# Attention output and adapters with head dims on partitions, sums of the softmax by a stationary matrix of ones

## The chip, the cores and the metric

One core of one Trainium2 chip runs the whole kernel. The metric is the device time of one execution in microseconds (us). The engines are TensorE (PE, with its weight loads PEld), VectorE (DVE), ScalarE (ACT), GpSimd (POOL) and SyncE (SP); each works through its own queue in order.

## What is computed

Banded attention for 8 batch rows, 8 heads, 576 positions and head size 64, and then a mixture of low-rank adapters on the 4608 resulting rows of 512 numbers:

```python
scores = scale * np.matmul(q, k.transpose(0, 1, 3, 2))
mask_plain = (rel >= 0) & (rel < window)                      # window 32, heads 0 to 3
mask_dil = (rel >= 0) & (rel < window * dilation) & (rel % dilation == 0)   # dilation 4, heads 4 to 7
attn = np.exp(scores - max)
attn = attn / (np.sum(attn, axis=-1, keepdims=True) + 1e-09)
x = np.matmul(attn, v)                                        # then to rows of 8 heads x 64
...
logits = x @ w_gate                                           # 8 experts
topk = np.argpartition(-logits, K, axis=1)[:, :K]             # the best 2
w = softmax over the two
delta[mask] += w[mask, k, None] * ((x[mask] @ A[e]) @ B[e])   # rank 16
return x + delta
```

## The kernel before

The host reorders q, k, v so that the dilated heads become banded heads too (positions sorted by their class modulo 4). A batch row is then two groups g of four heads, and within a group two pairs xy of two heads. Keys lie in 9 blocks of 64, and a block meets at most 96 queries, so a score tile has 64 keys on partitions and 96 queries along the row.

For each batch row r (there are 8) the steps are, by the names that the plan gives them:

- loads `g`, `q`, `v`: q, k and v of one group and half, from float32 in memory to bf16 in the tile `kv`, 64 partitions each, issued on POOL. Three slots of `kv` are used in turn.
- S0, S1: masks and scores of a group by small matmuls into two banks each; E0, E1: the exponential on ACT, from PSUM to the tile `p` (bf16). Keys are on partitions.
- Va, Vb (line 612): for a pair of heads, values. `p` is the stationary operand, 128 queries wide, and v of two heads is the moving one, 65 columns each: 64 of v and a column of ones that the host put there, whose product is the sum of the softmax. So the result has queries on partitions, and each query's sums are single columns. H (line 657) does the same for the last 64 positions of all eight heads.
- R and RH (lines 635, 677): the reciprocals of those columns on DVE; N and NH: the product of values and reciprocals, on DVE, from PSUM to the output tile `x` in float32. N frees the banks of the pair.
- B and BH: casts of `x` to bf16 on POOL (tiles `xb`, `xbh`). T0, T1, TH: transposes on PE by the identity, so that head dims lie on partitions; C0, C1, CH: copies of the transposes on ACT to the tile `xt`.
- Z0, Z1: gate and first adapter matrices, `xt` stationary; ZC: copies to `zs` on ACT; M, s12, tt, th, top, g2: the choice of the best two and their weights (DVE, and a tanh on ACT); gz: weighted products on POOL.
- GT: transposes of gz on PE; gc and gn: two copies of them, in class order on DVE and in natural order on ACT. D: the second adapter matrices, gn and gc stationary, `bt` moving; A: the addition to `x` on DVE. For the names in `VIA` the addition goes by a copy to `tmp` on ACT (AC) and an addition on POOL (AP).
- st: stores of finished columns of `x`, issued on SP behind the loads.

The order on every engine is written out by hand in the string `ORDER`. A name with `@n` also says which PSUM bank, of eight, it starts in. `replay` only reads it; the costs given to `add` (for example `dve(60)` for R) set nothing but the filler matmuls. Instructions are recorded by a wrapper, so all stand at line 124 in the profile; they are told apart by their tiles.

```python
ve.reciprocal(rec, o[:, :, D : D + VW + 1 : VW])        # R: 8 numbers per partition
...
ve.reciprocal(RECH[r % 2], o[:, :, D])                  # RH: 4 numbers per partition
```

Of the kernel before, what the change touches and what calls it, by code (L numbers as in the profile page):

```python
# [10 lines left out]
FP = mybir.dt.float32  # L11
# [13 lines left out]
PER = 192  # L25
CI = S // C
VW = D + 1
# [5 lines left out]
KV = 2 * VN + QN  # L33
# [17 lines left out]
VIA = ("4 4", "4 5", "4 6", "3 7")  # L51
GT2 = (7,)
# [3 lines left out]
startACT aw land_aw startPOOL startSP con land_con bt land_bt startDVE pz11 pz31 table pz10 g011 land_g011  # L56
zero00 g010 land_g010 q000 land_q000 zero10 btc q001 land_q001 v000 land_v000 v001 land_v001 md S0_0.1@0 pz20
pz00 g100 land_g100 E0_0.1 S1_0.1@2 zero01 Va_0.2@0 E1_0.1 Vb_0.2 g101 land_g101 pz01 xz1 awc S0_0.0@2 E0_0.0
R_0.2 xz0 N_0.2 g110 land_g110 pz21 g111 land_g111 gz00 g200 land_g200 S1_0.0@4 E1_0.0 Va_0.0@2 g201 land_g201
Vb_0.0 zero11 gz01 R_0.0 N_0.0 Va_0.3@4 Vb_0.3 R_0.3 N_0.3 Va_0.1@0 Vb_0.1 R_0.1 N_0.1 H_0@2 RH_0 g211  # L60
land_g211 S0_1.0@4 E0_1.0 g210 land_g210 S1_1.0@0 E1_1.0 B_0.0 pz30 B_0.2 NH_0 B_0.3 B_0.1 T1_0@3 C1_0 T0_0@2
Va_1.0@4 Va_1.1@6 g301 land_g301 C0_0 Vb_1.0 R_1.0 N_1.0 Vb_1.1 R_1.1 N_1.1 BH_0 TH_0@3 CH_0 S0_1.1@0 E0_1.1
g300 land_g300 Z0_0@3 ZC0_0 M0_0 g310 land_g310 Z1_0@6 ZC1_0 M1_0 zero20 S1_1.1@0 E1_1.1 s12_0 B_1.0 top_0
Va_1.2@2 tt_0 th_0 Va_1.3@6 g2_0 B_1.1 zero21 T0_1@4 C0_1 Vb_1.2 R_1.2 Vb_1.3 N_1.2 R_1.3 S0_2.0@0 E0_2.0
H_1@5 S1_2.0@2 gz0_0 E1_2.0 GT_0@4 Va_2.1@0 N_1.3 B_1.3 Va_2.0@6 RH_1 NH_1 BH_1 gc_0 gn_0 Vb_2.1 R_2.1 TH_1@2
CH_1 N_2.1 B_1.2 Vb_2.0 R_2.0 N_2.0 T1_1@3 C1_1 D2p_0@4 A2p_0 S0_2.1@0 E0_2.1 S1_2.1@6 g311 land_g311 E1_2.1
B_2.0 Z1_1@3 ZC1_1 M1_1 g400 land_g400 Z0_1@2 ZC0_1 M0_1 g401 land_g401 g410 land_g410 Va_2.3@4 Va_2.2@6
Vb_2.3 R_2.3 s12_1 g411 land_g411 top_1 B_2.1 N_2.3 B_2.3 Vb_2.2 R_2.2 S0_3.0@2 tt_1 N_2.2 H_2@0 RH_2 E0_3.0
NH_2 BH_2 S1_3.0@4 th_1 g2_1 T0_2@1 gz0_1 E1_3.0 C0_2 Va_3.1@2 D4_0@6 A4_0 Vb_3.1 R_3.1 N_3.1 B_3.1 Va_3.0@4
B_2.2 TH_2@0 CH_2 Vb_3.0 R_3.0 D0p_0@6 N_3.0 A0p_0 S0_3.1@2 E0_3.1 GT_1@0 g501 land_g501 g500 land_g500  # L70
S1_3.1@4 E1_3.1 g510 land_g510 T1_2@1 gc_1 gn_1 Va_3.2@6 Va_3.3@2 Vb_3.2 R_3.2 N_3.2 Vb_3.3 C1_2 D0p_1@4 A0p_1
R_3.3 N_3.3 B_3.0 T0_3@0 g511 land_g511 C0_3 Z0_2@1 ZC0_2 Z1_2@6 ZC1_2 M0_2 M1_2 s12_2 S0_4.0@4 E0_4.0 H_3@1
top_2 RH_3 NH_3 B_3.2 tt_2 S1_4.0@2 E1_4.0 D2p_1@6 A2p_1 B_3.3 T1_3@4 Va_4.0@0 C1_3 Va_4.1@2 BH_3 TH_3@5 CH_3
th_2 g2_2 Vb_4.0 R_4.0 N_4.0 Vb_4.1 R_4.1 N_4.1 S0_4.1@6 E0_4.1 Z0_3@5 ZC0_3 g601 land_g601 M0_3 Z1_3@4 ZC1_3
M1_3 s12_3 tt_3 S1_4.1@6 E1_4.1 top_3 th_3 gz0_2 GT_2@5 Va_4.3@2 gc_2 g2_3 Va_4.2@0 D4_1@4 A4_1 gn_2 Vb_4.3
R_4.3 N_4.3 Vb_4.2 g610 land_g610 R_4.2 N_4.2 S0_5.0@6 H_4@5 E0_5.0 RH_4 NH_4 S1_5.0@2 E1_5.0 gz0_3 GT_3@4
gc_3 gn_3 B_4.0 D0p_2@6 A0p_2 B_4.3 D2p_2@0 A2p_2 S0_5.1@2 E0_5.1 B_4.1 T0_4@5 Va_5.0@6 D4_2@4 A4_2 Vb_5.0
R_5.0 C0_4 g600 land_g600 S1_5.1@2 E1_5.1 Va_5.1@0 N_5.0 B_4.2 T1_4@5 C1_4 g611 land_g611 BH_4 TH_4@4 Vb_5.1
CH_4 R_5.1 N_5.1 Va_5.3@2 Va_5.2@6 Vb_5.3 R_5.3 N_5.3 Vb_5.2 D0p_3@4 A0p_3 R_5.2 g700 land_g700 Z0_4@0 Z1_4@1
ZC1_4 N_5.2 M1_4 ZC0_4 M0_4 top_4 B_5.3 s12_4 tt_4 g710 land_g710 B_5.2 S0_6.0@2 E0_6.0 H_5@4 RH_5 NH_5  # L80
S1_6.0@0 E1_6.0 S0_6.1@6 E0_6.1 D2p_3@2 A2p_3 T1_5@5 Va_6.1@0 g711 land_g711 g701 land_g701 B_5.1 BH_5 D4_3@4
A4_3 S1_6.1@6 B_5.0 Vb_6.1 C1_5 th_4 g2_4 gz0_4 Va_6.0@4 E1_6.1 R_6.1 N_6.1 TH_5@2 CH_5 T0_5@3 C0_5 Vb_6.0
R_6.0 N_6.0 Va_6.2@6 Va_6.3@0 GT_4@2 gc_4 gn_4 st_0 land_st_0 Vb_6.3 R_6.3 Vb_6.2 R_6.2 N_6.3 N_6.2 Z1_5@4
Z0_5@5 ZC1_5 M1_5 D4_4@0 ZC0_5 M0_5 S0_7.1@2 AC4_4 s12_5 tt_5 th_5 H_6@6 D2p_4@0 RH_6 NH_6 E0_7.1 S0_7.0@4
E0_7.0 S1_7.0@6 E1_7.0 top_5 A2p_4 D0p_4@2 g2_5 A0p_4 B_6.3 B_6.2 T1_6@0 C1_6 Va_7.0@4 BH_6 TH_6@1 Va_7.1@6 fz
Vb_7.0 R_7.0 B_6.1 Vb_7.1 CH_6 S1_7.1@2 E1_7.1 AP4_4 st_3 land_st_3 R_7.1 B_6.0 T0_6@1 gz0_5 N_7.1 N_7.0 C0_6
GT_5@0 gc_5 gn_5 B_7.0 Va_7.2@6 Va_7.3@2 Vb_7.2 R_7.2 Vb_7.3 R_7.3 N_7.2 N_7.3 Z0_6@1 ZC0_6 M0_6 B_7.1 Z1_6@0
ZC1_6 T0_7@6 C0_7 M1_6 s12_6 B_7.2 H_7@1 D4_5@0 RH_7 tt_6 B_7.3 T1_7@2 th_6 C1_7 NH_7 D2p_5@4 BH_7 TH_7@1 CH_7
top_6 g2_6 gz0_6 D0p_5@6 A2p_5 Z0_7@1 A0p_5 GT_6@4 gc_6 AC4_5 ZC0_7 Z1_7@5 ZC1_7 M0_7 gn_6 D2p_6@4 M1_7 s12_7
tt_7 th_7 top_7 g2_7 A2p_6 D4_6@1 AP4_5 AC4_6 st_5 land_st_5 D0p_6@6 A0p_6 gz0_7 gz3_7 GTn_7@6 gn_7 AP4_6 st_6  # L90
land_st_6 GT_7@7 gc_7 D3_7@7 AC3_7 D2_7@6 A2_7 st_7c land_st_7c D4_7@4 D0p_7@0 AP3_7 A4_7 st_7b land_st_7b
A0p_7 st_7a land_st_7a
# [234 lines left out]
def attn_adapters_kernel(  # L327
# [24 lines left out]
    XB = [[sb([128, 4, 128], BF, f"xb{i}{h}") for h in range(4)] for i in range(2)]  # L352
    XBH = [sb([128, 256], BF, f"xbh{i}") for i in range(2)]
# [3 lines left out]
    GN = [sb([128, 640], BF, f"gn{i}") for i in range(2)]  # L357
    GC = [sb([128, 640], BF, f"gc{i}") for i in range(2)]
    REC = [sb([128, 4, 2], FP, f"rec{i}") for i in range(3)]
    RECH = [sb([128, 4], FP, f"rech{i}") for i in range(2)]  # L360
# [8 lines left out]
    TMP = [sb([128, 512], FP, f"tmp{i}") for i in range(2)]  # L369
# [72 lines left out]
    for s in range(SLOTS):  # L442
        for a, (half, cols) in enumerate(((lo, slice(ROW, ROW + VN)), (hi, slice(QG, QG + VN)))):
            f = (dve, act, pool)[s]

            def emit(s=s, half=half, cols=cols):
                view = T[s][half, cols]
                if s == 1:
                    se.copy(view.bitcast(FP), T[0][half, cols].bitcast(FP))
                else:  # L450
                    (ve, None, ge)[s].memset(zero(view), 0)

            zeros[s, a] = add(
                **f(VN // 2), name=f"zero{s}{a}", prio=(-55, -25, -55)[s], emit=emit,
                deps=[zeros[0, a]] if s == 1 else [],
            )
    pz = []
    for i in range(NP):
        for a in range(2):
            gaps = P[i][:, a].rearrange("p (s c) -> p s c", c=PER)[:, :, SEG:PER]  # L460
            z = add(
                **dve(NB * SEG // 2), name=f"pz{i}{a}", prio=(-60, -54, -20, -10)[i] + a,
                emit=lambda gaps=gaps: ve.memset(zero(gaps), 0),
            )
            pz.append(z)
    gz0 = [add(
        **dve(64), name=f"gz0{i}", prio=-4,
        emit=lambda i=i: (ve.memset(zero(GC[i][:, 576:640]), 0), ve.memset(zero(GN[i][:, 512:576]), 0)),
    ) for i in range(2)]
# [21 lines left out]
    def load(r, half, c0, c1, deps, name):  # L491
        n = len(INST)
        INST[n] = None
        shift = 0 if half == 0 else QG + VN
# [12 lines left out]
    def vcols(half, g):  # L507
        base = (QG + (1 - g) * VG, ROW + g * VG)[half]
        return base, base + VG

    def qcols(half, g):
        base = ((1 - g) * (QG + VN), QG + VN + g * (QG + VN))[half]
        return base, base + QG
# [21 lines left out]

    pdone = {}
# [7 lines left out]
    def two_heads(r, g, xy, b):  # L544
        t = T[r % SLOTS]
        at = vcols(0, g)[0] + (xy * NB + b) * VW
        v = t[:, at : at + VW]
        return bass.AP(tensor=v.tensor, offset=v.offset, ap=[v.ap[0], [vcols(1, g)[0] - vcols(0, g)[0], 2], [1, VW]])

    def attention(r):  # L550
        for g in range(2):
# [8 lines left out]
            for part, (b0, nb) in enumerate(((0, 5), (5, 4))):  # L560
# [35 lines left out]
                def exps_(k=k, nb=nb, b0=b0, pb=pb):  # L596
# [7 lines left out]
                         deps=[sc] + pz[2 * (seq % NP) : 2 * (seq % NP) + 2] + pdone.get(seq - NP, []),  # L604
# [3 lines left out]
            for xy in range(2):  # L608
# [3 lines left out]
                def values(us, r=r, g=g, xy=xy, p=p, k=k):  # L612
                    for u in us:
                        o = pair(k)[:, u // 2, 256 * (u % 2) : 256 * (u % 2) + 2 * VW]
                        jobs = [(2 * u * PER, 2 * u), ((2 * u + 1) * PER - 64, 2 * u + 1)]
                        if u:
                            jobs.append(((2 * u - 1) * PER + 64, 2 * u - 1))
                        for n, (at, b) in enumerate(jobs):
                            te.matmul(
                                o, lhsT=p[:, xy, at : at + 128], rhs=two_heads(r, g, xy, b),  # L620
                                start=(n == 0), stop=(n == len(jobs) - 1), skip_group_check=True,
                            )
# [368 lines left out]
```

## Time and profile before

| what | us |
|---|---|
| median of 11 runs | 101.54 (101.2 to 102.78) |
| the profiled execution | 102.11 |
| its span, first to last instruction | 100.3 |
| PE busy in it | 78.4 |
| DVE busy | 71.1 |
| ACT busy | 64.6 |
| POOL busy | 54.6 |
| first reciprocal starts | 12.39 |
| last load of q, k, v lands | 75.45 |
| last instruction of DVE ends | 95.8 |

The span is that of one profiled execution. A busy time is the time in which the engine had an instruction in work. A group of the profile gives an operation, its output and input tiles, its shape (partitions x elements), the number of instructions, and after the bar the busy time, the mean duration in ns and the idle time of the engine just before it. The granted clock of TensorE was 0.99 of full speed.

### The profile page before, as it was taken

The page shows a single profiled execution, that of the slowest core. Times are in us where ns is not written, and L with a number is a line of the kernel's source. Part 1 is how long each engine was busy: PE and PEld are TensorE (multiplying, and loading weights), DVE is VectorE, ACT ScalarE, POOL GpSimd, SP SyncE. Part 2 cuts the span into 40 slices and gives each one's busy share as a digit, 9 for nine tenths or more (in the row PEclk, how much of TensorE's full clock was granted, in tenths as well). Part 3 has the DMA queues.
Part 4 walks back from the last instruction along what each step waited for, and adds up shares of the span by engine and source line. Part 5 has one row for each costly group of instructions (what it writes and reads, how often), then busy time and mean ns, then how long its engine had stood idle before and what let it go on. Part 6 is the DMA issues. An engine that isn't in the chain of part 4 may idle for free.

```text
span 100.3 us, 3719 instructions
## 1 busy us (share of the span) xinstructions
PE 78.4 (78%) x1561; PEld 63.6 (63%) x1561; DVE 71.1 (71%) x208; ACT 64.6 (64%) x113; POOL 54.6 (54%) x92
## 2 busy tenths in 40 slices
PE   0033867789898998999987989998999999988400
PEld 0012546678785976897866769876966997653300
DVE  5873057554759498689694996999789889987620
ACT  5420873499887665789792888299669879642200
POOL 5923344987582939943357850477149466541400
PEclk9999999999999999999999999999999999999995
DMA  2999999999999999999999999999969898996892
GB/s 46 315 208 196 215 213 217 219 211 208 220 208 223 208 211 220 208 220 216 214 212 205 223 197 213 192 144 162 197 227 518 356 440 357 463 374 257 369 360 110
DMA packets 4176, 24.50 MB, mean 244 GB/s; under 512 B 832, under 2 KB 832, under 8 KB 3648
## 3 DMA queue, kind: packets, MB, share of 16 engines
q0 software_dynamic: 2720, 14.23, 70.9%
q1 hardware_dynamic: 1296, 9.76, 23.7%
q10 hardware_dynamic: 144, 0.28, 0.8%
q8 instruction: 12, 0.20, 0.7%
q14 instruction: 4, 0.03, 0.1%
HBM read 29.06 MB, written 9.44 MB: 384 GB/s over the span
## 4 chain that ended last, share of the span: by engine, by line
PE 34%; DMA 33%; DVE 9%; ACT 6%; issue 6%; POOL 6%; DVEq 1%; ACTq 0%; POOLq 0%
PE ps L124 34%; DMA kv<-in_rows_dram 33%; DVE x L124 7%; ACT xt L124 4%; POOL kv L124 4%; POOL xb L124 2%; ACT p L124 1%; ACT gn L124 1%; DVE rec L124 1%; DVEq L981 0%; ACT zs L124 0%; POOL xbh L124 0%; ACT th L124 0%; DVE mx L124 0%; DVE tt L124 0%
## 5 line engine op out<-in xcount | busy, mean ns | idle before, releaser
L124 ACT ACTIVATE p<-ps 128x960 bf16<-128x960 f32 (+1 forms) x32 | 27.6, 895 | 15.9 <-PE ps L124 15.0
L124 PE MATMUL ps<-kv,p 128*128 128x130 bf16 (+1 forms) x416 | 29.7, 223 | 3.2 <-issue 1.5
L124 POOL CAST xb<-x 128x512 bf16<-128x512 f32 x32 | 19.4, 619 | 20.1 <-DVE x L124 20.0
L124 PEld LDWEIGHTS <-p 128*128 128x128 bf16 (+1 forms) x416 | 23.7, 99 | 5.7 <-ACT p L124 2.1
L124 DVE TENSOR_TENSOR x<-ps,rec 128x512 f32<-128x512 f32 x32 | 21.7, 686 | 0.8
L124 DVE TENSOR_TENSOR x<-x,ps 128x1024 f32<-128x1024 f32 (+2 forms) x21 | 20.4, 1000 | 2.6 <-PE ps L124 2.3
L124 POOL DMA_DIRECT2D kv<-in_rows_dram x34 | 17.9, 539 | 6.4 <-DMA kv<-in_rows_dram 5.3
L124 ACT COPY xt<-ps 128x1024 bf16<-128x1024 bf16 (+1 forms) x32 | 19.2, 650 | 1.4 <-PE ps L124 1.1
L124 PE MATMUL ps<-kv 64*64 64x96 bf16 (+1 forms) x576 | 13.0, 208 | 4.2 <-DMA kv<-in_rows_dram 4.1
L124 PEld LDWEIGHTS <-kv 64*64 64x64 bf16 x576 | 11.5, 111 | 7.5 <-DMA kv<-in_rows_dram 5.6
L124 DVE RECIPROCAL rec<-ps 128x8 f32<-128x8 f32 x32 | 6.5, 204 | 12.8 <-PE ps L124 12.2
L124 POOL TENSOR_TENSOR gz<-zs,g 128x640 bf16<-128x640 f32 (+1 forms) x8 | 9.8, 1219 | 7.2 <-DVE g L124 7.1
L124 PE MATMUL ps<-aw,xt 128*128 128x136 bf16 x160 | 11.0, 223 | 0.6 <-ACT xt L124 0.6
L124 PE MATMUL ps<-md,con 64*64 64x480 bf16 (+1 forms) x64 | 6.6, 388 | 5.5 <-DVE md L124 5.1
L124 PEld LDWEIGHTS <-con 64*64 64x64 bf16 x128 | 4.3, 106 | 10.1 <-DMA con<-in_con_dram 3.7
L124 PEld LDWEIGHTS <-xt 128*128 128x128 bf16 x160 | 9.7, 98 | 1.1 <-ACT xt L124 1.0
L124 PE MATMUL ps<-bt,gn 128*128 128x256 bf16 x40 | 9.7, 274 | 0.9 <-ACT gn L124 0.9
L124 PE MATMUL ps<-con,xb 128*128 128x128 bf16 x128 | 9.6, 219 | 0.1
L124 PE MATMUL ps<-bt,gc 128*128 128x256 bf16 x40 | 9.7, 273 | 0.0
L124 ACT COPY zs<-ps 128x408 f32<-128x408 f32 (+1 forms) x16 | 6.7, 444 | 3.9 <-PE ps L124 3.7
L124 PEld LDWEIGHTS <-xb 128*128 128x128 bf16 x128 | 7.7, 98 | 0.7 <-issue 0.4
L124 ACT COPY gn<-ps 128x512 bf16<-128x512 bf16 (+1 forms) x16 | 5.6, 408 | 3.7 <-PE ps L124 2.5
(39 smaller groups left out, 73.9 us busy)
## 6 DMA issues: line engine op xcount, KB each, us to landing
kv<-in_rows_dram POOLq DMA_DIRECT2D x30, 434.2 KB, 10.9
out_dram<-x SPq DMA_DIRECT2D x1, 3456.0 KB, 11.6
out_dram<-x SPq DMA_DIRECT2D x1, 2304.0 KB, 12.2
out_dram<-x SPq DMA_DIRECT2D x2, 1152.0 KB, 5.4
kv<-in_rows_dram POOLq DMA_DIRECT2D x2, 288.0 KB, 8.4
out_dram<-x SPq DMA_DIRECT2D x1, 512.0 KB, 3.1
out_dram<-x SPq DMA_DIRECT2D x1, 384.0 KB, 2.3
kv<-in_rows_dram POOLq DMA_DIRECT2D x2, 146.2 KB, 9.3
```

The lines of the kernel that those rows point to most:

```text
L124: i = call(*args, **kw)
```

## The change

The result of the attention gets head dims on partitions and positions along the row, from the values on.

- Va, Vb and H: v of two heads is now the stationary operand, read from `kv` at a step of 18 elements, and `p` is the moving one, at most 96 columns. The sums are made by further matmuls with a stationary 128x128 tile `ob`, ones in its two 64x64 diagonal blocks: every one of the 64 partitions of a head gets the same sum. A pair of banks then holds values in its first bank and sums in its second.
- R and RH take the reciprocal of all of that: 128x512 and 128x256. N and NH multiply two full tiles.
- T, TH, C, CH and the tiles `xb`, `xbh` go. The casts B and BH on POOL write `xt` themselves (for the plain heads with a permuted read, and BH in two instructions).
- GT turns into one copy, gc, on ACT; gn and the second transposes of the last row go. D has `bt` as the stationary operand and gc as the moving one, up to 512 columns.
- `VIA` has the additions of the first two heads' pairs (128x1024) of rows 0 to 6 on ACT and POOL, in place of three of 128x256; that of the last row's fourth tile stays there.
- The ones column of v goes from the host's data, v is stored with head dims outside and blocks inside, and the two halves of a group lie next to each other in `kv`. The gaps of `p`, gc and gn need no zeros. `ORDER` is a new list with the same kinds of steps.

```diff
-PER = 192
+PER = SEG
-VW = D + 1
+VW = D
-VIA = ("4 4", "4 5", "4 6", "3 7")
-GT2 = (7,)
+VIA = ("0p 0", "0p 1", "0p 2", "0p 3", "0p 4", "0p 5", "0p 6", "3 7")
...
+    SC = [sb([128, 512], FP, f"sc{i}") for i in range(3)]
+    OB = sb([128, 128], BF, "ob")
+    SCH = [sb([128, 256], FP, f"sch{i}") for i in range(2)]
...
+    def ones():
+        ve.memset(zero(OB), 0)
+        for a in range(2):
+            ve.memset(OB[64 * a : 64 * a + 64, 64 * a : 64 * a + 64], 1.0)
...
+    def NORM(dst, sums, o):
+        ve.tensor_tensor(dst, o, sums, ALU.mult)
...
     def two_heads(r, g, xy, b):
...
+        at = vcols(0, g)[0] + xy * NB + b
+        step = 2 * NB
+        return T[r % SLOTS][:, at : at + 127 * step + 1 : step]
...
-                            te.matmul(
-                                o, lhsT=p[:, xy, at : at + 128], rhs=two_heads(r, g, xy, b),
-                                start=(n == 0), stop=(n == len(jobs) - 1), skip_group_check=True,
-                            )
+                    for b in range(5) if first else (5, 6, 7):
+                        n = min(SEG, 512 - 64 * b)
+                        te.matmul(
+                            o[:, 0, 64 * b : 64 * b + n], lhsT=two_heads(r, g, xy, b), rhs=p[:, xy, SEG * b : SEG * b + n],
+                            start=(b == 0), stop=(b == 7), skip_group_check=True,
+                        )
...
+                    for n, (dst, src) in enumerate(jobs):
+                        te.matmul(dst, lhsT=OB, rhs=src, start=(first and n == 0), stop=(n == 2), skip_group_check=True)
...
-                def recip(k=k, rec=rec):
-                    o = pair(k).rearrange("p b (u n) -> p (b u) n", u=2)
-                    ve.reciprocal(rec, o[:, :, D : D + VW + 1 : VW])
+                def sums(k=k, sc_=sc_):
+                    ve.reciprocal(sc_, pair(k)[:, 1])
+
+                def norm(k=k, sc_=sc_, r=r, hp=hp):
+                    NORM(X[:, r, 512 * hp : 512 * hp + 512], sc_, pair(k)[:, 0])
...
-                    ge.tensor_copy(XB[r % 2][hp], X[:, r, 0:2048].rearrange("p (u h n) -> p u h n", u=4, h=4)[:, :, hp])
+                    src = X[:, r, 512 * hp : 512 * hp + 512]
+                    if hp < 2:
+                        ge.tensor_copy(
+                            XT[r % 2][:, hp, 0:S].rearrange("p (c i) -> p c i", c=C)[:, :, 0:128],
+                            src.rearrange("p (i c) -> p c i", c=C),
+                        )
+                    else:
+                        ge.tensor_copy(XT[r % 2][:, hp, 0:512], src)
...
-            ve.reciprocal(RECH[r % 2], o[:, :, D])
+            ve.reciprocal(SCH[r % 2], bank(k)[:, 256:512])
...
-        gc = add(**dve(290), emit=lambda k=k: ve.tensor_copy(GC[i][:, 0:S], bank(k).bitcast(BF)[:, 0:S]),
+        gc = add(**act(S), emit=lambda k=k: se.copy(GC[i], bank(k).bitcast(BF)[:, 0:S]),
...
+                        src = natural[:, 0:128] if h < 2 else GC[i][:, 0:512]
...
+                    te.matmul(dst, lhsT=BT[:, 128 * h : 128 * h + 128], rhs=src, start=True, stop=True, skip_group_check=True)
```

## The prediction

> **What bounds the kernel now.** I read the page's head first: busy times, slices, transfers. The first fence shows that no engine fills the span. TensorE is busiest (78%), VectorE (DVE) has 71.1 us of work and 29 us of idle time. The 16 DMA engines are the fullest resource: nine tenths or more in nearly every slice, at some 210 GB/s written during the loads and above 350 GB/s at the stores.
>
> ```profile
> span 100.3 us, 3719 instructions
> PE 78.4 (78%) x1561; PEld 63.6 (63%) x1561; DVE 71.1 (71%) x208; ACT 64.6 (64%) x113; POOL 54.6 (54%) x92
> DMA  2999999999999999999999999999969898996892
> q0 software_dynamic: 2720, 14.23, 70.9%
> PE 34%; DMA 33%; DVE 9%; ACT 6%; issue 6%; POOL 6%; DVEq 1%; ACTq 0%; POOLq 0%
> ```
>
> The last of these lines is the chain of waits that ended last: it alternates between TensorE and the loads of q, k, v, and DVE has 9% of it. So a microsecond saved on DVE is worth little today, and DVE has 29 us to give before it decides. Whether the change stays inside that is the question, because it turns DVE's smallest instruction into one of its largest. So next I read the groups of instructions with shapes kept apart, then the tile of the reciprocals:
>
> ```profile
> L124 DVE TENSOR_TENSOR x<-ps,rec 128x512 f32<-128x512 f32 x32 | 21.7, 686 | 0.8
> L124 DVE TENSOR_TENSOR x<-x,ps 128x1024 f32<-128x1024 f32 x15 | 18.0, 1216 | 0.3 <-issue 0.2
> L124 DVE RECIPROCAL rec<-ps 128x8 f32<-128x8 f32 x32 | 6.5, 204 | 12.8 <-PE ps L124 12.2
> L124 DVE TENSOR_TENSOR x<-ps,rech 128x256 f32<-128x256 f32 x8 | 3.3, 415 | 0.2
> L124 DVE RECIPROCAL rech<-ps 128x4 f32<-128x4 f32 x8 | 1.4, 171 | 0.0
> ```
>
> ```profile
> L124 DVE RECIPROCAL rec<-ps x32: 189/207/209, 12.4 to 81.5; 128x8 f32<-128x8 f32 x32
> L124 DVE TENSOR_TENSOR x<-ps,rec x32: 639/691/693, 12.7 to 82.2; 128x512 f32<-128x512 f32 x32
> L124 DVE RECIPROCAL rech<-ps x8: 168/172/175, 18.2 to 83.5; 128x4 f32<-128x4 f32 x8
> L124 DVE TENSOR_TENSOR x<-ps,rech x8: 361/424/425, 18.8 to 83.7; 128x256 f32<-128x256 f32 x8
> ```
>
> Durations stand as minimum/median/maximum in ns. The multiplication gains 691 - 424 = 267 ns for 256 more elements, 1.04 ns each. The reciprocal gains 207 - 172 = 35 ns for only four more, 8.75 ns each (by the means 33 / 4 = 8.25). Is the larger one dearer because it reads two banks with one more dimension? The multiplications do the same, two banks against one, and both have the same fixed part: 691 - 512 x 1.04 = 424 - 256 x 1.04 = 158 ns. So I read the 35 ns as a price per element, eight of the multiplication's (8 x 1.04 = 8.3), on a fixed 138 ns.
>
> **The change part by part.** *The reciprocals.* Before, R takes 8 sums per partition and RH 4, since queries lay on partitions. Now the sums are replicated over 64 head dims, and R takes 128x512, RH 128x256, in the same 32 + 8 instructions. With 8.34 ns: R = 138 + 512 x 8.34 = 4.41 us, RH = 138 + 256 x 8.34 = 2.27 us. Sum 32 x 4.41 + 8 x 2.27 = 141.1 + 18.2 = 159.3 us against 7.9 now. Bounds: by the multiplications of the same size (one element per step) 32 x 0.686 + 8 x 0.415 = 25.3 us; by the medians' 8.75 ns 32 x 4.62 + 8 x 2.38 = 166.9 us. I take 159.3, since the nearest rows are those of the same operation.
>
> The Trainium skill has a rule on each side. "VectorE: DVE Perf Modes", section "First, the fixed hardware budget", says that the reciprocal is an iterative divide with a repeat count of 8; at one pass per multiplication step that estimates 512 x 8 x 1.04 ns = 4.3 us per R and some 156 us in all. "Vector Engine (DVE) Microarchitecture Reference", section "Measured stream behaviour on trn2", says that built-in one- and two-source ops need 1.0417 ns per column plus about 75 ns; an estimate by that is 0.61 us per R and some 22 us in all. The two rows above agree with the first.
>
> *The rest of DVE.* The 32 N and 8 NH keep their sizes (22.0 + 3.3 us). Seven of the 128x1024 additions go to ACT and POOL; 8 stay (8 x 1.216 = 9.7), with eight of 128x256 in place of five (8 x 0.416 = 3.3) and one of 128x512 (0.7). The copies gc leave (3.6). The gate's small operations stay (MAX8 4.1; s, tt, top, g 7.2; gz 0.4). Of the memsets, those of p, gc and gn leave, and about 4.2 us stay. Sum without reciprocals 54.9 us; with them 214.2. Neighbours overlap: in the timeline R starts at 55.34, N at 55.58, RH at 56.18, so the pair takes 0.84 where its durations add up to 0.89; over 40 pairs that is 2 us. DVE needs 212.2 us, more than twice today's span.
>
> *TensorE*, hidden from here on: 144 transposes of x and 5 of gz leave (8 take 0.5 us in the timeline, so 9 us); 512 small matmuls make values and sums where 416 did (22 take 1.4 us, so +6); 80 matmuls of 256 columns become 32 of 512 and 32 of 64, about equal. Net some -2 us of 78. The stationary v is read at a step of 18 elements; no row shows such a weight load. Bounds: 97 ns (the contiguous one), or a whole 128x130 pass more each; over 288 loads that is 0 to +64 us, all of it beside 212 us of DVE. *ACT* loses 32 copies xt (19.8 us), 16 of gn (6.5), three of tmp (1.2), gains 8 of gc (about 0.59, as gn's 128x512: 4.7) and 7 of tmp (1.02, as xt's 128x1024: 7.1): 64.6 to about 49. *POOL* keeps 32 casts, half now with a permuted read (0.62 to, at worst, gz's 1.27 us each: up to +10), casts the end in two pieces (+3), loses three additions of 128x256 (2.2) and gains seven of 128x1024: 128x256 took 0.73 and 128x512 1.27, so 2.34 each, 16.4. So 54.6 to some 72 to 82. *DMA*: each partition's row falls from 6948 to 6912 elements, 0.5% or 0.35 us; DMA counts and queues stay. The cover of all these edits is DVE's own queue: 26 us per batch row. Without it each would count at its price against today's 100 us.
>
> *What waits where.* R is queued on DVE ahead of N, and N is what frees the two banks and what the casts (B) and so the adapters wait for. Everything behind R in DVE's queue (gate, additions) is late by the same 4.4 us, and PE waits for banks. But PE, ACT and POOL need only 6 to 10 us per row, and the written order mostly has the next head's values ahead of N, so DVE should seldom run dry. I grant 1 us per row (8 in all) for heads whose values stand in PE's queue behind a matmul that waits for the bank just freed, and for tanh between tt and g. Bounds: 1 us in all, and 24 (3 per row, a score, exponential and value stretch).
>
> *The sum.* The first R starts at 12.39 now; the new order has the scores of the second group and the next Va ahead of that Vb (some 0.7 us): 13.1. DVE after it: 212.2 - 3.9 (memsets that lie before it) = 208.3. Idle 8. At the end the last row's gate and adapters run with DVE partly idle (tanh, gz on POOL, transposes, gc, the last matmuls). Between 87 and 95.8 us DVE's gaps are some 2 us today and two additions of 128x1024 (2.35 us) fill another; in the new order one of 128x256 (0.42) stands there, so I take 3.5. From DVE's end to the span's end 4.45 us today (95.8 to 100.3). 13.1 + 208.3 + 8 + 3.5 + 4.45 = 237.4 us of span. The profiled execution took 102.11 around a span of 100.3, so 239.2; it was 0.6 above the median of 101.54. Forecast: 239 us.
>
> **The rivals.** *One element per step.* If the reciprocal streams like a multiplication, R is 0.69 us and DVE sums to 54.9 + 25.3 = 80 us. Place: R on DVE; it decides below about 1 us per R, where DVE's 29 us of slack cover it. Then the loads still set the pace (0.35 us sooner) and the tail loses the copies of xt and gn (some 2 us): 99.5 us, faster. For it: only the two tiny shapes are known. Against: the 35 ns. *Weights at a step.* If strided loads of v cost far more than a pass, PE passes DVE's 26 us per row once each of 36 exceeds some 0.5 us ((26 - 8) / 36). At 1 us each a row takes 8 + 36 = 44 us: some 370. For it: no row shows such a read; against: so large a factor. *Hand to hand.* If banks make DVE and PE alternate at each head, scores, exponentials and values (some 3.1 us, 9.16 to 12.27 in the early timeline) add to each of 32 heads: 99 us more, about 338. For it: N frees banks; against: four pairs of banks, and R of one head beside Vb of another in the order.
>
> **How the numbers follow.** Forecast 0.87, one element per step 0.07, weights 0.03, hand to hand 0.03. The forecast's ends: idle 1, the lower slope (-1.8) and a shorter tail (-2.5) give about 228, with 2 us for the start 226; the upper slope (+7.6) and 24 us of idle (+16) give 262. About nine tenths of the forecast's 0.87 lie inside, which is near 8 in 10. Half a per cent is what a measurement of this kernel can tell from no change. Faster 0.05 and same 0.01 come from the streaming rival, whose last hundredth is slower; slower 0.94.
>
> **What would show it.** Right: RECIPROCAL 128x512 near 4.4 us and 128x256 near 2.3, DVE above 85% busy with some 212 us, the chain of waits mostly DVE, DMA idle in most slices, PE and POOL waiting for DVE. Wrong: a 128x512 reciprocal below 1 us; weight loads from kv of 0.5 us or more; DVE idle for more than 30 us behind PE.

## The result, and the profile after

The changed kernel takes 196.14 us (median of 12 runs, 194.9 to 196.94) against 102.05 us for the kernel before (47 runs): 1.926 times as long, interval 1.921 to 1.931. Here and below a time is the median of all runs, while ratios and their intervals leave out executions that fell in a slower state. The forecast was right that it is much slower, and that DVE decides; its 239 us, and the low end of its range (226), were too high.

The page's head of the profiled execution (195.47 us, span 193.7): first the busy times, then the busy tenths in 40 slices of the span, then the granted TensorE clock and the DMA share in the same slices, then the chain of waits that ended last.

```profile
span 193.7 us, 3535 instructions
...
PE 118.7 (61%) x1492; PEld 80.9 (42%) x1492; DVE 171.0 (88%) x189; ACT 54.1 (28%) x79; POOL 78.9 (41%) x106
...
DVE  4419999999899999979999999999999989999831
...
PEclk9999555795557585558556655599576756955596
DMA  6999993185050222991874035335508800190574
...
DVE 68%; PE 22%; DMA 4%; issue 3%; ACT 1%; POOL 0%; ACTq 0%; DVEq 0%; POOLq 0%
```

DVE went from 71% to 88% and from 9% to 68% of the chain. DMA, which was full in nearly every slice, is below a tenth in seven of the 40 (the forecast's sign was "idle in most slices"). A span that doubled while PE's share fell is the picture of one engine that everyone waits for. The groups of DVE with shapes kept apart say which instruction it is (busy us, mean ns of one, idle time before it):

```profile
L121 DVE RECIPROCAL sc<-ps 128x512 f32<-128x512 f32 x32 | 107.2, 3350 | 8.5 <-PE ps L121 8.5
L121 DVE TENSOR_TENSOR x<-ps,sc 128x512 f32<-128x512 f32 x32 | 21.9, 684 | 0.9
L121 DVE RECIPROCAL sch<-ps 128x256 f32<-128x256 f32 x8 | 13.8, 1727 | 0.0
```

The reciprocals are 107.2 + 13.8 = 121.0 us, where they were 7.9. The multiplications beside them have not changed (684 ns, and 686 before). The waits (who waited for whom: us in total, times, longest us) show the other engines behind DVE, and DVE behind nobody for long:

```profile
POOL xt L121 <- DVE x L121: 76.7, 26, 5.8
PEld L121 <- DVE x L121: 58.8, 33, 4.1
PE ps L121 <- DVE x L121: 55.9, 30, 3.6
...
DVE sc L121 <- PE ps L121: 8.5, 5, 6.1
```

Last, DVE by stretches of time (length, busy us and instructions, granted clock, DMA share, GB/s):

```profile
0.00:20.00 20.00, 10.24 (x21) 0.99 0.95 203
20.00:60.00 40.00, 38.55 (x31) 0.62 0.54 103
60.00:100.00 40.00, 38.21 (x41) 0.59 0.53 101
100.00:140.00 40.00, 39.67 (x41) 0.67 0.41 68
140.00:180.00 40.00, 38.50 (x45) 0.67 0.35 148
180.00:194.00 14.00, 5.77 (x15) 0.74 0.62 253
```

From 20 to 180 us DVE is idle for 160 - 154.9 = 5 us. All the rest of its idle time lies at the two ends.

### The profile page after: what moved, and what is told of

Read it like the earlier page. It is cut to its first block, busy times and chain, and to the rows that moved or that the text cites. A ratio compares the mean times of both kernels' runs of the same rounds, so it can differ in the third digit from the quotient of the medians.

```text
span 193.7 us, 3535 instructions
## 1 busy us (share of the span) xinstructions
PE 118.7 (61%) x1492; PEld 80.9 (42%) x1492; DVE 171.0 (88%) x189; ACT 54.1 (28%) x79; POOL 78.9 (41%) x106
## 4 chain that ended last, share of the span: by engine, by line
DVE 68%; PE 22%; DMA 4%; issue 3%; ACT 1%; POOL 0%; ACTq 0%; DVEq 0%; POOLq 0%
DVE sc L121 50%; PE ps L121 22%; DVE x L121 10%; DVE sch L121 5%; DMA kv<-in_rows_dram 4%; DVE s L121 1%; DVE mx L121 1%; ACT p L121 1%; DVE tt L121 0%; POOL kv L121 0%; ACT gc L121 0%; DVE g L121 0%; DVE top L121 0%; ACT th L121 0%; ACTq L121 0%
## 5 line engine op out<-in xcount | busy, mean ns | idle before, releaser
L121 DVE RECIPROCAL sc<-ps 128x512 f32<-128x512 f32 x32 | 107.2, 3350 | 8.5 <-PE ps L121 8.5
L121 PEld LDWEIGHTS <-kv 64*64 64x64 bf16 (+1 forms) x896 | 44.6, 149 | 51.3 <-DVE x L121 28.4
L121 POOL CAST xt<-x 128x512 bf16<-128x512 f32 (+1 forms) x48 | 32.3, 692 | 80.1 <-DVE x L121 76.7
L121 PE MATMUL ps<-p,kv 128*128 128x96 bf16 (+2 forms) x320 | 35.9, 249 | 27.0 <-DVE x L121 24.8
L121 PE MATMUL ps<-gc,bt 128*128 128x512 bf16 (+1 forms) x64 | 25.9, 524 | 16.7 <-DVE x L121 16.4
L121 PE MATMUL ps<-p,ob 128*128 128x96 bf16 (+4 forms) x192 | 32.5, 271 | 0.0
L121 DVE TENSOR_TENSOR x<-ps,sc 128x512 f32<-128x512 f32 x32 | 21.9, 684 | 0.9
L121 POOL TENSOR_TENSOR x<-x,tmp 128x1024 f32<-128x1024 f32 (+1 forms) x8 | 17.7, 2223 | 3.0 <-ACT tmp L121 3.0
L121 PEld LDWEIGHTS <-ob 128*128 128x128 bf16 x192 | 17.9, 126 | 0.0
L121 DVE RECIPROCAL sch<-ps 128x256 f32<-128x256 f32 x8 | 13.8, 1727 | 0.0
## 6 DMA issues: line engine op xcount, KB each, us to landing
out_dram<-x SPq DMA_DIRECT2D x1, 3456.0 KB, 11.5
```

The costliest lines, as they stand in the source:

```text
L121: i = call(*args, **kw)
```

## The experiments

Theory: DVE's queue sets the time, and the reciprocal costs a fixed part and a price per element that the forecast put too high. The first rivals: something else in the new kernel (the order, PE) takes a large part; or the price depends on the layout, the type or the source.

### The reciprocals as copies of the same size

```diff
-                    ve.reciprocal(sc_, pair(k)[:, 1])
+                    ve.tensor_copy(sc_, pair(k)[:, 1])
...
-            ve.reciprocal(SCH[r % 2], bank(k)[:, 256:512])
+            ve.tensor_copy(SCH[r % 2], bank(k)[:, 256:512])
```

> The changed kernel with both reciprocals replaced by plain copies of the sums of the same sizes (128x512 and 128x256, PSUM to SBUF, VectorE); the output is values times sums. Theory (the element price of the reciprocal is the whole loss): 121 us of reciprocals become some 22 to 25 us, VectorE's busy time falls from 171 to about 73, the loads set the pace again, 98 to 106 us. Rival (TensorE has a price of its own in this layout: weights read at a step, granted clock 0.68, 22% of the chain): the time stays above 115 us, with weight loads from kv well above the 97 ns of the contiguous ones of before.

Measured: 116.5 us, 1.146 times the kernel before (1.132 to 1.160). Of the 94 us, 80 leave with the reciprocals, and 14 stay: more than the theory allowed (106 us), and on the rival's side of 115, with weight loads from `kv` at a mean of 153 ns. So the theory was not complete. Whether the weights are the rest is tried further down. The head of this kernel's page has PE, not DVE, with the largest share of the chain (last line):

```profile
span 114.2 us, 3535 instructions
...
PE 90.4 (79%) x1492; PEld 62.4 (55%) x1492; DVE 85.0 (74%) x189; ACT 52.8 (46%) x79; POOL 79.3 (69%) x106
...
PE 44%; DVE 26%; POOL 9%; DMA 7%; ACT 5%; issue 4%; POOLq 0%; ACTq 0%; DVEq 0%
```

Two things in it looked odd. In PE's tile view the matmuls of D (duration minimum/median/maximum in ns) reach 1044 ns, and in the timeline one of DVE's smallest instructions lasts 2.76 us:

```profile
L121 PE MATMUL ps<-gc,bt x64: 190/334/1044, 31.8 to 108.0; 128*128 128x512 bf16 x32, 128*128 128x64 bf16 x32
```

```profile
57.14 2.76 DVE L121 TENSOR_TENSOR top<-zs,mx 128x40 f32<-128x40 f32 x1
59.82 0.16 DVE L121 TENSOR_TENSOR s<-mx 128x5 f32<-128x5 f32 x1
```

```profile
57.45 2.38 POOL L121 TENSOR_TENSOR x<-x,tmp 128x1024 f32<-128x1024 f32 x1
```

The timeline's columns are start and duration in us. The DVE instruction ends at 57.14 + 2.76 = 59.90, POOL's addition at 57.45 + 2.38 = 59.83; a step later the 128x5 instruction takes 0.16. So the small one seems to end only with POOL's. It is not alone: ten of the gate's small instructions (`s`, `tt`, `top`) last more than 0.8 us in this trace, and nine of them end within 0.07 us of an addition of POOL (four) or of one of its casts to `xt` (five). The Trainium skill's page "SBUF — State Buffer", section "Who interferes with whom", has a rule for this: a DVE instruction with two inputs in SBUF contends with a GpSimd instruction that reads SBUF, the ports that they share are an exclusive lock, and the order of issue decides who blocks. The trace agrees on the contention. On the order it agrees in eight of the ten, where an instruction of POOL that computes was running when DVE's began; in the case shown above DVE's has the earlier start (57.14 against 57.45) and is held all the same, for a reason that these rows do not show. Three more kernels, further down, price both oddities.

### Half of the columns

```diff
-                    ve.reciprocal(sc_, pair(k)[:, 1])
+                    ve.reciprocal(sc_[:, 0:256], pair(k)[:, 1, 0:256])
+                    ve.tensor_copy(sc_[:, 256:512], pair(k)[:, 1, 256:512])
```

(RH in the same way, 128 and 128 columns.)

> The changed kernel with the reciprocal taken of the first half of the columns only (128x256 and 128x128) and a copy for the other half; half of the output is not divided. Theory: VectorE's queue is the bound, so the time follows its sum: per head 3.35 becomes 1.75 + 0.42, per row 1.73 becomes 0.93 + 0.29, in all -42 us, 154 us. Rival (something beside VectorE holds the end, as the TensorE clock): less than that comes back, above 165 us.

Measured: 150.31 us, 1.484 (1.465 to 1.503). The page's head and DVE's groups:

```profile
span 148.1 us, 3575 instructions
...
PE 100.7 (68%) x1492; PEld 68.7 (46%) x1492; DVE 124.6 (84%) x229; ACT 53.6 (36%) x79; POOL 79.0 (53%) x106
```

```profile
L121 DVE RECIPROCAL sc<-ps 128x256 f32<-128x256 f32 x32 | 56.0, 1749 | 9.9 <-PE ps L121 9.7
```

DVE's sum falls by 171.0 - 124.6 = 46.4 us and the span by 193.7 - 148.1 = 45.6: one for one, and the time is near the 154 us that the theory gave. That is what a bound engine looks like. It speaks against a rival that puts a large part of the added time on something beside DVE's queue.

### The kernel before, with the same reciprocals added for nothing

```diff
                     ve.reciprocal(rec, o[:, :, D : D + VW + 1 : VW])
+                    ve.reciprocal(JUNK.rearrange("p (u n) -> p u n", u=4), o[:, :, 0:128])
...
             ve.reciprocal(RECH[r % 2], o[:, :, D])
+            ve.reciprocal(JUNK[:, 0:256].rearrange("p (h n) -> p h n", h=4), o[:, :, 0:64])
```

> The kernel before with an extra reciprocal of 128x512 behind each R and of 128x256 behind each RH, written to a scratch tile that nothing reads; nothing else changed. Theory: the same 121 us on VectorE do the same in the old layout: 71 + 121 = 192 us busy, first one at 12.4 us, about 210 us of time. Rival (the new layout or its order is what costs): clearly below the changed kernel's 196 us.

Measured: 213.54 us, 2.101 (2.079 to 2.124). DVE's groups in it:

```profile
L124 DVE RECIPROCAL junk<-ps 128x512 f32<-128x512 f32 x32 | 105.9, 3309 | 0.0
...
L124 DVE RECIPROCAL junk<-ps 128x256 f32<-128x256 f32 x8 | 13.8, 1724 | 0.0
```

The two groups add up to 119.7 us. Neighbours overlap more in this kernel, and the multiplication N behind them counts 635 ns in place of 686, so DVE's busy time grew by less, from 71.1 to 181.5, by 110.4. The span grew from 100.3 to 212.5, by 112.2. So DVE's 29 us of idle time in the kernel before took up nothing of it: DVE is idle for 31 us here. The likely reason, not tried by itself, is that this idle time is spread over waits for other engines, and work that comes behind such a wait does not slide into the gap. The reciprocals alone are enough to double the old kernel; nothing else of the change is needed.

### The price of a reciprocal by itself

A series of reciprocals behind all other work of the kernel before (one execution, 164.96 us):

```diff
+        for again in range(3):
+            for n in (512, 4, 64, 8, 256, 16, 128, 32):
+                ve.reciprocal(J[:, 0:n], one_bank[:, 0:n])
+            ve.reciprocal(J[:, 0:8].rearrange("p (u n) -> p u n", u=4), two[:, :, D : D + VW + 1 : VW])
...
+            ve.reciprocal(J[:, 0:512], X[:, 7, 0:512])
...
+                ve.reciprocal(JB[:, 0:512], one_bank)
...
```

> The kernel before with a series of reciprocals and multiplications behind its last addition, three times each, to read their durations; they lengthen the end. Theory: one straight line through the two sizes of the changed kernel, 144 + 6.26 n ns: 169 (n 4), 194 (8), 545 (64), 3349 (512), and the old R's 207 ns for eight numbers are its shape (eight single columns in two banks), dearer than eight neighbours. Rival 1: the first elements are dearer, so eight neighbours also take about 207 and four 172. Rival 2: the price depends on the source or type, so SBUF or bf16 has another slope.

DVE's groups (junk is the target of the added ones, rech the kernel's own RH):

```profile
L124 DVE RECIPROCAL junk<-ps 128x512 f32<-128x512 f32 x3 | 10.1, 3355 | 0.1
L124 DVE RECIPROCAL junk<-x 128x512 f32<-128x512 f32 x3 | 10.1, 3353 | 0.1
...
L124 DVE RECIPROCAL junkb<-ps 128x512 bf16<-128x512 f32 x3 | 9.9, 3305 | 0.0
...
L124 DVE RECIPROCAL junk<-ps 128x256 f32<-128x256 f32 x3 | 5.3, 1757 | 0.1
...
L124 DVE RECIPROCAL junk<-ps 128x8 f32<-128x8 f32 x9 | 1.9, 207 | 0.3
L124 DVE RECIPROCAL junk<-ps 128x64 f32<-128x64 f32 x3 | 1.7, 557 | 0.1
L124 DVE RECIPROCAL rech<-ps 128x4 f32<-128x4 f32 x8 | 1.4, 171 | 0.0
L124 DVE RECIPROCAL junk<-ps 128x4 f32<-128x4 f32 x6 | 1.1, 182 | 0.2
```

From 8 to 512 elements: (3355 - 207) / 504 = 6.246 ns each; 64 gives 157 + 64 x 6.25 = 557, 256 gives 1757, 4 gives 182. A straight line, 157 ns and 6.25 ns per element, which is six of the multiplication's 1.04 ns. PSUM or SBUF, float32 or bf16, 128 or 64 partitions (3350), eight neighbours or eight single columns in two banks (in the same group, 207): all the same within 50 ns. So layout, type, source and a dearer first element fall as causes. The theory of this run missed in one point: it had eight neighbours at 194 ns and took the 207 ns of the old R for the price of its shape; both take 207, and the fixed part is 157 ns, not 144. What misled the forecast stands in the last two rows: four elements cost 182 ns in a series, but 171 in the kernel's own RH (median 172 in the trace that the forecast used). Those 10 ns, divided by the four elements between RH and R, are the 2.5 ns by which 8.75 is above 6.25. Why RH takes 171 ns in its place in the kernel is not shown. That a short instruction's duration moves with its neighbours is: R, the same instruction, has a mean of 204 ns in the kernel before and of 192 with a second reciprocal behind it.

### What the 14 us without reciprocals are

Three kernels on top of the one with copies. D with its moving operand unstrided (its columns then come out in class order for all heads):

```diff
-                        src = natural[:, 0:128] if h < 2 else GC[i][:, 0:512]
+                        src = GC[i][:, 0:512]
```

> The copy kernel of e1, with the second adapter matmuls of the plain heads reading gc in its stored order instead of at a step of 144 elements, so their columns come out in class order. In e1 such a matmul of 512 columns was followed by the next one after 849 ns, the one that reads neighbours after 216. Theory (what is left above the kernel before is partly TensorE's strided moving operand): 16 x 0.63 = 10 us of TensorE go, and as it has 44% of e1's chain, 6 to 10 us of the time: 106 to 111. Rival (hidden): 115 to 118.

POOL's additions (AP) cut to 8 columns, so that most of this work is left out:

```diff
-                    ge.tensor_tensor(v, v, TMP[j][:, 0:n], ALU.add)
+                    ge.tensor_tensor(v[:, 0:8], v[:, 0:8], TMP[j][:, 0:8], ALU.add)
```

> The copy kernel of e1, with the additions on GpSimd (AP) cut to 8 columns; most of these additions are left out. In e1 a 128x5 multiplication or addition of VectorE that reads only SBUF took up to 1.5 us and one of 128x40 2.76 us, and ended with GpSimd's instruction. Theory (VectorE's small SBUF-only operations wait for GpSimd's long ones, in the chain of the gate): s falls from a mean of 1051 ns to about 0.2 us, top likewise, VectorE's busy time by 10 us, the time by 4 to 9 us: 107 to 112. Rival (GpSimd's work is hidden): s and top stay, 115 to 118.

Both, and v as stationary operand read densely (other elements of `kv` than v needs):

```diff
-        return T[r % SLOTS][:, at : at + 127 * step + 1 : step]
+        return T[r % SLOTS][:, vcols(0, g)[0] + 128 * (b % 4) : vcols(0, g)[0] + 128 * (b % 4) + 128]
```

> e5 and e6 together, and v read as neighbours in the stationary operand (wrong elements of v). Theory: the three prices explain what e1 has above the kernel before, 97 to 104 us. If the two edits alone did nothing and this does, it was the strided weights (153 against 97 ns each in e1). Rival (the written order or the banks are what holds): 110 or more.

| kernel | us | against the kernel before | PE, DVE busy us |
|---|---|---|---|
| copies | 116.5 | 1.146 (1.132 to 1.160) | 90.4, 85.0 |
| with D unstrided | 111.36 | 1.088 (1.076 to 1.100) | 81.0, 85.4 |
| with short additions on POOL | 109.77 | 1.063 (1.048 to 1.078) | 89.5, 77.5 |
| with both and dense weights | 103.4 | 1.015 (1.010 to 1.020) | 74.2, 77.4 |

D in the second kernel, where its longest matmul falls from 1044 to 393 ns:

```profile
L121 PE MATMUL ps<-gc,bt x64: 190/334/393, 31.7 to 103.1; 128*128 128x512 bf16 x32, 128*128 128x64 bf16 x32
```

DVE's small instructions in the third (they took 1051 and 594 ns with the copies alone):

```profile
L121 DVE TENSOR_TENSOR s<-mx 128x5 f32<-128x5 f32 x8 | 5.0, 623 | 0.2
...
L121 DVE TENSOR_TENSOR top<-zs,mx 128x40 f32<-128x40 f32 x8 | 1.5, 191 | 0.0
```

So some 5 us is the strided moving operand (5.1 by the medians, 5.9 by the ratios), a little less than the 6 to 10 that were expected, and some 7 us (6.7, or 8.5 by the ratios) the large additions on POOL, part of it by `top` and `s`. The forecast of 0.2 us for `s` was missed: it still took 623 ns. The trace of this kernel says beside what (columns as in the timeline above):

```profile
46.98 1.12 POOL L121 CAST xt<-x 128x512 bf16<-128x512 f32 x1
47.22 0.90 DVE L121 TENSOR_TENSOR s<-mx 128x5 f32<-128x5 f32 x1
```

Five of the eight `s` last 0.83 to 1.01 us here, and each ends 0.02 to 0.04 us after such a cast; the other three take 0.16 or 0.17. So it seems to be the casts to `xt` that hold `s`, as the additions held `top`. The two edits' gains add up to 11.8 us, that is 104.7. If they do add up, dense weights are worth the 1.3 us to 103.4, or nothing by the ratios, which is within what these runs can tell apart. In the last kernel the loads fill DMA again. Its windows have the stretch and its length, busy us of PE, PEld, DVE, ACT and POOL, then the granted clock, the DMA share (0.97 and 1.00) and GB/s:

```profile
0.00:50.00 50.00, 33.56 (x738) 25.46 (x739) 35.42 (x86) 26.11 (x38) 33.29 (x57) 1.00 0.97 198
50.00:95.00 45.00, 40.68 (x758) 29.40 (x756) 40.72 (x103) 26.27 (x41) 29.18 (x50) 1.00 1.00 291
```

In DMA and clock this is the kernel before's picture. The chain that ended last is another: DVE has 39% of it and DMA 9%, where the kernel before has 9% and 33%. Even with the reciprocals gone and three other costs taken out, the change is 1.5% behind. What these 14 us cost in the changed kernel was not measured. DVE is idle there for only 9.1 us after its first R, so most of it can only lie under the reciprocals; `s` shows a little, 8 x 514 ns.

### A version with the division on another engine

All of RH, and 28 of the 32 R, as exp(-ln) on ACT, with ln and exp in one loaded set; sigmoid by exp and ln in place of tanh; gc and the additions of `VIA` (but the last row's) back on DVE.

```diff
-                    ve.reciprocal(sc_, pair(k)[:, 1])
+                    if hp == 3 and r % 2:
+                        ve.reciprocal(sc_, pair(k)[:, 1])
+                        return
+                    se.activation(sc_, pair(k)[:, 1], AF.Ln)
+                    se.activation(sc_, sc_, AF.Exp, scale=-1.0)
```

> The changed kernel, all of the computation kept, with the reciprocals as exp(-ln) on ACT (two instructions of 128x512; 28 of 32 and all eight small ones; four stay on VectorE), the tanh as exp and ln of the same table set, and gc and the additions 0p back on VectorE. Theory (the reciprocal's place is the whole gap between 196 and e1's 116.5): ACT about 89 us busy, VectorE about 75, TensorE 90, 108 to 120 us. Rival (values that are really divided cost elsewhere too): above 140.

Measured: 155.26 us, 1.512 (1.492 to 1.533): better than the changed kernel, but far from what was expected (108 to 120), and on the rival's side of 140. Its first wait, and ACT's two steps:

```profile
DVE x L121 <- ACT sc L121: 40.4, 20, 8.6
```

```profile
L121 ACT ACTIVATE sc<-sc 128x512 f32<-128x512 f32 x28 | 17.7, 631 | 0.9
L121 ACT ACTIVATE sc<-ps 128x512 f32<-128x512 f32 x28 | 16.6, 593 | 17.6 <-PE ps L121 17.6
```

No engine is above 72% busy here (PE; ACT 54%, DVE 50%). The engines' sums (PE 109.5 us at a clock of 0.87, ACT 82.4, DVE 76.2) would all fit into 120 us; what the expectation left out is the waits: `N` now waits for two ACT steps. That these stand in ACT's queue behind exponentials which were placed for a kernel without them is a reading of the list; the last run below tries it.

### The order

The changed kernel with the planner's own order in place of the written one, and with R and RH at 3080 and 1540 in the plan's cost:

```diff
-ORDER = """
...
+ORDER = ""
...
-                rc = add(**dve(512), emit=sums,
+                rc = add(**dve(3080), emit=sums,
```

> The changed kernel in an order and with banks that the kernel's own planner lays out, told that R costs 3.3 us and RH 1.7 us on VectorE, instead of the written list, which counted 0.6 and 0.35. Nothing else changed. Theory (VectorE's sum of 171 us is the bound, not the order): 188 to 200 us. Rival (a list made for cheap reciprocals loses by itself): below 185.

Measured: 183.7 us, 1.811 (1.803 to 1.820): outside the theory's 188 and on the rival's side of 185, so the written list does cost 12 us against this plan. But the bound has not moved. DVE between 50 and 90 us, and its `s`, in this kernel:

```profile
50.00:90.00 40.00, 40.00 (x44) 0.82 0.47 90
```

```profile
L86 DVE TENSOR_TENSOR s<-mx 128x5 f32<-128x5 f32 x8 | 1.7, 207 | 0.0
```

DVE has no idle time at all there. Its sum is 162.5 us (171.0 with the list); 2.4 us of the 8.5 are `s`, at 207 in place of 514 ns. The first R starts at 11.34 in place of 13.93 us. After its first R, DVE has 158.0 us of work where it had 166.75: that and the earlier start, 8.7 + 2.6 = 11.3, are nearly all of the 11.9 us by which the span fell. The plan also puts in more filler matmuls (PE has 1667 in place of 1492), and the granted clock is 0.84 in place of 0.68; what of the gain comes with them and what from the order was not tried apart.

The version on ACT with the planner's order:

> e8 (28 of 32 reciprocals and the small ones as exp(-ln) on ACT) in an order that the planner lays out for that. Theory (e8's 155 us with no engine above 72% busy came from a list that had R on VectorE, so that N waits behind ACT's other work, 40 us in all): 110 to 130. Rival (the two steps on ACT and the banks they hold are the delay whatever the order): 145 or more.

Measured: 137.93 us (135.87 to 138.51), beside 101.57 of the kernel before. It lies between the two expectations. A good part of the delay in the version on ACT was the list. What holds the rest was not settled: in this trace N still waits 24.7 us for ACT's two steps (40.4 with the list), and PE has 44% of the chain. No version that was tried beats the kernel before.

## Why the prediction was right, and where it was wrong

| step | forecast us | measured us |
|---|---|---|
| first R starts | 13.1 | 13.9 |
| 40 reciprocals | 159.3 | 121.0 |
| DVE's other work | 52.9 | 50.0 |
| of both, before the first R | 3.9 | 4.2 |
| DVE idle after its first R | 8 + 3.5 | 9.1 |
| DVE's end to the span's end | 4.45 | 3.9 |
| span | 237.4 | 193.7 |

The measured column is 13.9 + (121.0 + 50.0 - 4.2) + 9.1 + 3.9 = 193.7. The step that failed is the price in "So I read the 35 ns as a price per element, eight of the multiplication's (8 x 1.04 = 8.3), on a fixed 138 ns". It is six, on a fixed 157: 3350 ns per R where 4.41 us were forecast. That is 38.3 us of the 43.7 by which the span was missed. The other rows together miss by 5.4 us. With the 121.0 us that were measured the same sum gives 239.2 - 38.3 = 201 us, against 195.47 for the profiled execution.

Two shapes four elements apart cannot carry a slope: an error of 10 ns in one of them, 6% of its duration, made the price a third too high (8.34 for 6.25), since it was divided by 4 and then multiplied by 512. The forecast's own row warned of it: R, one shape, ran from 189 to 209 ns there, a spread of more than half of the 35 ns. And the range did not own up to it. The forecast took its lower slope from the means of the same two rows (8.25), which share the error, and took its low side from idle time and the tail; a fixed part like the multiplication's 158 ns, which stood in the same paragraph, would have given (204 - 158) / 8 = 5.75 ns, R = 3.10 and RH = 1.63 us, and 239.2 - (159.3 - 112.3) = 192 us for the low side.

The number eight seemed backed by the Trainium skill's page "VectorE: DVE Perf Modes", section "First, the fixed hardware budget", with its repeat count of 8. The runs measure six steps per element at every size, so the count is not a price in steps of the multiplication. The rule on the other side, one column per 1.0417 ns on the page "Vector Engine (DVE) Microarchitecture Reference", section "Measured stream behaviour on trn2", fails by far more: 0.61 us against 3.35.

Point by point. *The bound*: right. DVE is 88% busy, has 68% of the chain, and time follows its sum one for one (half of the columns). *The rest of DVE*: right within 3 us. *Idle 8 us and an end of 3.5*: 9.1 together, where 11.5 was granted; the written order did keep DVE fed. That the order was good enough does not mean that it was good: the planner's own, with its fillers, saves 12 us. *POOL 72 to 82 us*: 78.9. *ACT about 49*: 54.1, with gc (639 ns) close to the 0.59 forecast. The 5 us are durations that were taken off a busy time in which they overlapped: ACT's groups of the kernel before add up to 70.7 us where its busy time is 64.6. *TensorE, hidden*: the mean strided weight load of 128x128 from `kv` takes 155 ns in the changed kernel (320 of them, where the forecast counted 288) and 153 with the copies alone, where dense ones take 100 in the last of the three kernels, so near the low bound. But "80 matmuls of 256 columns become 32 of 512 and 32 of 64, about equal" was wrong: those of the plain heads take up to 1044 ns, and PE's busy time falls by 9.4 us when they are unstrided. In the changed kernel it lay under DVE, as the forecast had said of all of TensorE's edits.

*The rivals.* "One element per step" needed R below about 1 us; R is 3.35. Its own price, 99.5 us, was wrong too: with copies at that very speed the kernel takes 116.5, because of costs that the forecast had put under DVE's cover and did not price for the case without it. "Weights at a step" and "hand to hand" fall by the rows above: 155 ns, and 5 us of idle time in 160.

## What to carry to other kernels

A reciprocal cost 6.25 ns here for every element along the row that it was applied to: take it of the few sums before they are replicated, not of the matrix. A price per element needs two shapes that lie far apart, and where only close ones are in the trace, the range must take in the error of their difference times the factor to which it is stretched. When an engine covers other costs, price them once without the cover: here they were 14 us, enough to turn the best case from a gain into a loss.

## What the runs showed of the hardware

- DVE's reciprocal in a series: 157 ns and 6.25 ns per element along the row, from 4 to 512 elements; PSUM or SBUF, float32 or bf16 and 128 or 64 partitions change it by at most 50 ns.
- Tiny DVE instructions with both inputs in SBUF lasted until an addition or a cast of POOL ended: 2.76 us in one place, where the mean of the same instruction is 0.19 with POOL's additions cut short. A DVE addition of 128x1024 with one input in PSUM took its usual 1.21 us beside the same kind of POOL addition (at 54.22 us with the copies).
- A moving operand in bf16 whose columns lie 144 elements apart (four of them, then the next four one element on): up to 1044 ns for 512 columns, against at most 393 when dense.
- TensorE's granted clock was 0.68 in the changed kernel, 0.86 with half of the reciprocals and 0.98 with none, where PE was busy for 61%, 68% and 79% of the span. The same 1492 matmuls count 118.7, 100.7 and 90.4 us in these. The busy share alone does not say the clock: it was 0.99 at 73% in the last of the three kernels and 0.84 at 82% with the planner's order. In the series of reciprocals the clock was 1.00 from 70 to 96 us, with PE busy for 24.1 of the 26, and 0.50 from 110 us on, where no matmul ran.
